# Gated mix of infini-attention and a ReGLU block: PV of two head groups in one stretch, with a new order of all instructions

## The chip, the cores and the metric

The kernel runs on one core of a Trainium2 chip. A core has five engines with instruction queues of their own: PE (matmuls; its weight loads are listed apart as PEld), ACT (ScalarE), DVE (VectorE), POOL (GpSimd) and SP (SyncE, which here only issues DMAs). The metric is the device time of one execution in microseconds (us), median of the runs.

## What is computed

x has 2048 tokens of 512 features. One branch is an attention with 32 heads of 16 features in four segments of 512 tokens, causal within a segment, with a compressive memory of the earlier segments; the other is a ReGLU block of width 1792. A gate per token mixes them.

```
scale, phi = 16 ** -0.5, lambda t: where(t > 0, t + 1, exp(t))
for s in range(4):                       # segments of 512 tokens; q, k, v = x@wq, x@wk, x@wv
    p     = softmax(q[s] @ k[s].T * scale + causal mask)
    a_dot = p @ v[s]                     # "PV"
    a_mem = (phi(q[s]) @ M) / (phi(q[s]) @ z + 1e-6)
    o[s]  = sigmoid(beta) * a_mem + (1 - sigmoid(beta)) * a_dot
    M, z  = M + phi(k[s]).T @ v[s], z + phi(k[s]).sum()
a = concat(o) @ wo
b = (relu(x @ W_gate) * (x @ W_up)) @ W_down
g = sigmoid((x * gate_w).sum(-1))
out = g * a + (1 - g) * b
```

## The kernel before

All data are bf16, sums in PSUM are f32. x is kept transposed on chip (xT, loaded in four chunks of 512 tokens, one per segment). For each segment there are projections (q, k, v: full 128x128 matmuls of 512 columns, L543 to L552), the score, PV, the memory, the ReGLU's wg and wu (L745) with relu (L753 on ACT, L754 on DVE) and product (hm, L756 on DVE), and the output tiles (wo, L777, and wd, L784, summed in one PSUM bank, then scaled on the way out, L793 and L794).

*Score visit* ("quad"). The 32 heads are four groups G of eight. The keys of a group stand in eight blocks c of 64 keys; a block is scored against the queries from 64c on, with four 32-row tiles of PE side by side, one per pair of heads (L653). Parts are packed so that each visit fills four PSUM banks with 512 columns: blocks 1 and 7, 2 and 6, 3 and 5, block 0 alone, and block 4 of two groups together. That gives nine visits per two groups, 72 in all. One ACT instruction (L657) takes the exponential of all four banks into a tile of E, and frees the banks for the next visit. POOL then masks the diagonal part of each block (L662, two instructions per part, 256 in all).

*PV* ("pv", L685). For one group, 128 matmuls read its E tiles and the values (vaug, and vsh, the same values shifted by 64 partitions) on 64-row tiles, into two PSUM banks. DVE transposes both banks (Tn, L695), and divides and gates (rden L702, rdg L704, ad L706), transposes back (L709 or L711), and in segments 1 to 3 adds the memory's part (L712), into oT, which wo reads.

*PSUM*: eight banks of 512 f32. Before, four (psL) belong to the score and four (psA) to everything else: a full matmul's tile takes one of them, a PV two, and is freed by its reader on ACT or DVE. *E*: eight tiles, seven in a ring and one for block 4.

*Order*. The order of every engine's instructions is written out: ORDER is a string of letters, each letter names a queue of instructions (score, PV, projections, each kind of eviction, loads and so on), and the next instruction of that queue is placed. BANKS gives the PSUM bank of each tile. Waits between engines follow from the order and from who reads and writes what. An engine runs its list strictly from the front, so an instruction that waits holds up all behind it on that engine. SP issues all loads and stores in its listed order; it also waits there.

The rows below use these names: psL/psA (ps after the change) for PSUM, E for exponentials, Tn/adT/oT for the steps behind PV, rl and hT for relu and product, osb for output tiles, Mbd for the memory.

Of the kernel before, what the change touches and what calls it, by code (L numbers as in the profile page):

```python
# [12 lines left out]

LAT = 60.0
# [10 lines left out]
    "hafgbgbgfgbgfgbgfagbfagbhhghbhhhhhihbjijbtttbttttbthhhhhbhthtijhtbttijttbttcttbttttDbttttCtbtttDtbtCbtbtFtbctIbItFbtbFJqbJtzJJtbEtxbtStGbvtGbzTvJtbMTq"  # L25
    "HtbJxvSbvSvbMvvcToqkvbLvoxtMTvbTvGTvlLvboqvoxvVMTvTvMTvTnlqVnvLoTvlxTMtWTtMmtTWtCTpqFvlSxtJtVJvTCvTtMyTVtTRqFvRtxvMTvJvpMvKTtSqzCvTTvMxTteMtrSeFTqATvx"
    "TvJetATttMeDTqJvxATtRvETvTvMyTqrAMTvxVQvAtrMUVUzATqUtAxTtpATtUtGTtHATqGvTxTvAtRtAvdHqMTtxTvATtTJttCTLqTvEKTtToxvdtvMTptCvTtSLqTErxSvAVtAtzTtTCvVTqATvM"
    "xtAdtRvEtLotdqAvpxCTtvTETvvTMKvTJqLvATxTvMvTdtMrzoqTpAvTxWvAvWMvtALTtAtHAqHvTAxTvosuPTMunTuPnpPqTuTxoXuTusuPuPTqPTOuTpJxuJTuuuXTquTxTsYuTPtPtPuTHXqTNu"
    "xYusvPuyPTuPTupTyRqXuuxSuTSvrNLTRqYuATxTJvATvvJvATvRLqvAxSuovMTvpTuMLvTqTArxuVQTvAUrUMTVBquATxuToutATpvTqSvxuATVtMTvUGvTOqVAvMTxvUAvYvJvMTKqTvoxvvMTpv"
    "TeMvTvTALvTeMqTvxTMvevBvMroeMTnqnvTxpATvvTAvovMTvATqLMvTxTvAvpMsvPtALtPTqADvTTxvPTtBtMrFTqTKJWvAxtWvAvtMvTDAtMTqTtAxtRtETvCtTtAvFtATLqTtBxtCTXttEtTsHu"  # L30
    "TPPTuPTqvXxJuJupvuMTquTxTsuTPuPtPtOTXqTGsxvPuPYPvuXyTMvTqTyRuuovxuTMpurRRqTAuxTtATuTJvtNKTuTGYTuATvouLqAprAxrQAUuUAUuBqtATxvUAtTouvHApqTAuxuuATTNuTvTB"
    "YvvMTLqTovxuMTvvuMnTqnpuToxJsuJPTuPvTPuTqTOvTvxYTMvpvMvvMTqvTxvMvsMvvTPqPTLvPTxvTvMvrMTqTAvTxvTAvMvvALTqAvxAvvMTTvMvTqTArTxMvBWAvWvTLAqTvxTAvAMTvvAvLq"
    "TAvTxMvTvTBvvMXTqvMTxTvXMTuuTquTxTuTuusvTPuPTMquxPuNXuuTqYrTxTTvAuAuTvTAuTLAqvAxuTAuuNTqYvTxTvMTvuMuTuTqrxvAuAvTuTAvTAvAqLuTxvuvNuYTuTvTMqTvMxvMvuuMTs"
    "qTPuPxTvPTuvXvMTvTvMTvTvLuqvxvMvvBvMTqvTAxuMvvNvLTvBYqrMTxTTvAvAvLTvTMvTvATLvAqAvxMvvAwMvTvBvMTwLTvTvvMvwLwrvAwAwwAwAvAwMwwAwwBwwwOwYOwwYwwwwwwOwwwYww"
    "wwwwwOwwwwwYNY"
)
BANKS = (
    "012312301230123023012302130231201320132013201301230210321032102310231023023020302013120312131213212301230213021301303120312031201201212012302301231231"
    "02020132032301230123012310231021230230120121302023023023102130213023023021"
# [31 lines left out]
class Epoch:  # L71
    _n = 0

    def __init__(self, nb=1):
        self.nb = nb
        self.group = (self,)
        Epoch._n += 1
        self.res = f"ACCep{Epoch._n}"
        self.bank = None
        self.readers = []  # L80
# [31 lines left out]
class Sched:  # L112
    ENGS = ("pe", "act", "dve", "pool", "sp")

    def __init__(self, ndma=16, nbanks=4):
# [89 lines left out]
    def place(self, op, e, banks):  # L205
        op.eng = e
        if op.ep is not None and op.ep.bank is None:
            assert op.role == "w"
            for ep in op.ep.group:
                bi = next(banks)  # L210
# [88 lines left out]
def build_kernel(nc, A_x, A_wq, A_wk, A_wv, A_wo, A_beta, W_g, W_u, W_d, gate_w, out):  # L299
# [7 lines left out]
    with contextlib.ExitStack() as stack:  # L307
        for name, shape, dt in plan(S, D, F):
            T[name] = stack.enter_context(nc.sbuf_tensor(name, shape, dt))
        PL = stack.enter_context(nc.psum_tensor("psL", [128, 4, 512], F32))  # L310
        PA = stack.enter_context(nc.psum_tensor("psA", [128, 4, 512], F32))
        for st in sc.streams:
            sc.sem[st] = stack.enter_context(nc.semaphore(f"s_{st}"))
        program(sc, nc, T, PL, PA, A_x, A_wq, A_wk, A_wv, A_wo, A_beta, W_g, W_u, W_d, gate_w, out, NSEG, KT, NF, NT, EPS, SCALE)
# [5 lines left out]
def program(sc, nc, T, PL, PA, A_x, A_wq, A_wk, A_wv, A_wo, A_beta, W_g, W_u, W_d, gate_w, out, NSEG, KT, NF, NT, EPS, SCALE):  # L320
# [5 lines left out]
    def pe(fn, occ, **k):  # L326
        k.setdefault("lat", PE_LAT)
        if k.get("role") == "w":
            k["reads"] = list(k.get("reads", ())) + [f"init{i}" for i in range(4)]
# [17 lines left out]
    def A(ep):  # L347
        return PA[:, ep.bank, :] if ep.nb == 1 else PA[:, ep.bank:ep.bank + 2, :]

    def xt(c):  # L350
        return [f"xT{c}_{kt}" for kt in range(KT)] if c else [f"xT0_{kt}{h}" for kt in range(KT) for h in range(2)]
# [32 lines left out]
    def load_x(c):  # L384
        for kt in range(KT):
            lsp.append(dma("sp", lambda e, c=c, kt=kt: e.dma_start_transpose(V.xT[:, kt, c * 512:(c + 1) * 512], A_x[0, c * 512:(c + 1) * 512, kt * 128:(kt + 1) * 128]),
                           1 << 17, occ=1350.0, writes=[f"xT{c}_{kt}"], name=f"ldx{c}_{kt}"))
# [22 lines left out]
    for c in range(2, NSEG):  # L410
        load_x(c)
        for t in lsp[-KT:]:
            t.after = 36500.0 + 76000.0 * (c - 2)
    sc.queue(3, lsp)

# [15 lines left out]
    for b in range(4):  # L431
        ds.append(dve(lambda e, b=b: e.memset(PA[:, b, :], 0.0), 500, writes=[f"init{b}"], name=f"init{b}"))
# [4 lines left out]
    def warm(m, n, k, b):  # L437
        def fn(e):
            for i in range(m):
                ins = e.matmul(PL[:, b, 0:n], lhsT=nc.const_aps.tensor(1.0, [128, 128], BF16), rhs=nc.const_aps.tensor(1.0, [128, n], BF16), start=True, stop=True)  # L440
            return ins
        return pe(fn, m * n * (0.834 if k == 0 else 0.5), writes=[f"bankL{b}"], name=f"warm{k}")

    xps, xcs = [warm(5, 512, 0, 3)], []
    for h in range(2):
        for i in (2 * h, 2 * h + 1):
            for kt in range(KT):
                def fx(e, i=i, kt=kt):
                    return e.matmul(PL[:, kt, 128 * (i % 2):128 * (i % 2) + 128], lhsT=V.hT[:, i, kt * 128:(kt + 1) * 128], rhs=V.ident[:], start=True, stop=True)  # L449
                xps.append(pe(fx, 60 if h else 85, reads=[f"hT{i}", "ident"], writes=[f"bankL{kt}"], name=f"xt{i}_{kt}"))  # L450
                if h:
                    xps[-1].after = 5400.0
        for kt in range(KT):
            src, dst = PL[:, kt, 0:256], V.xT[:, kt, 256 * h:256 * h + 256]
# [441 lines left out]
```

## Time and profile before

| what | us |
|---|---|
| median of 3 runs (lowest, highest) | 264.38 (264.2, 265.23) |
| the profiled execution: span, first to last instruction | 262.5 |
| median less span (start and end around it) | 1.9 |
| busy: PE, DVE, ACT, POOL | 254.5, 189.2, 186.2, 122.7 |

The profile is of one execution. For that execution its span is known; its own device time is taken as span plus the 1.9 us of the table. Times in the views are us from the start of the span, durations of one instruction ns. Matmuls overlap in their rows, so the distance between two starts is what a matmul takes of PE, not the length in its row. "L653" is line 653 of the kernel before.

### The profile page before, as it was taken

Reading aid. Unit: us, or ns where it says so; the run is one execution under the profiler, and the core shown is the slowest. Engines: PE = TensorE matmul, PEld = TensorE weight load, DVE = VectorE, ACT = ScalarE, POOL = GpSimd, SP = SyncE. Lnnn points to the kernel's source line nnn. Section 1 sums busy time; section 2 is a strip of 40 time slices with the busy share of each in tenths; the row PEclk is TensorE's granted clock in tenths of the full one; section 3 lists DMA queues with packets and bytes.
Section 4 is the critical chain, followed back from the end, with each engine's and each line's share of the span. In section 5 each row is a group of like instructions: output and inputs, shape, how many; then the busy total and the mean of one; then the engine's idle time right before and its main releaser. Section 6 shows DMA issues by size and latency. Waiting matters only on the chain.

```text
span 262.5 us, 6602 instructions
## 1 busy us (share of the span) xinstructions
PE 254.5 (97%) x2727; PEld 115.2 (44%) x2761; DVE 189.2 (72%) x365; ACT 186.2 (71%) x163; POOL 122.7 (47%) x283
## 2 busy tenths in 40 slices
PE   8999999999999999999999999999999999999996
PEld 4644344434444444434444444444434444444444
DVE  4589878888894697888785898758973665577600
ACT  3698889888886977877876957777876755674021
POOL 3017645862655546845444456535654543343000
DMA  6999621342642312431212211010231000000011
GB/s 195 274 329 216 135 59 29 83 159 46 218 107 43 82 42 49 94 82 22 57 33 60 61 45 40 20 24 4 46 81 21 31 13 20 20 22 0 2 40 42
DMA packets 34685, 19.36 MB, mean 74 GB/s; under 512 B 24032, under 2 KB 34144, under 8 KB 34656
## 3 DMA queue, kind: packets, MB, share of 16 engines
q1 hardware_dynamic: 34272, 18.67, 27.7%
q8 instruction: 22, 0.36, 0.6%
q10 hardware_dynamic: 384, 0.27, 0.3%
q14 instruction: 7, 0.06, 0.1%
HBM read 9.87 MB, written 2.11 MB: 46 GB/s over the span
## 4 chain that ended last, share of the span: by engine, by line
PE 94%; issue 2%; DMA 1%; ACT 1%; SPq 0%; DVE 0%
PE psA L745 37%; PE psA L784 19%; PE psA L552 9%; PE psL L653 9%; PE psA L685 7%; PE psA L550 5%; PE psA L777 5%; PE psA L543 1%; DMA wq<-in_A_wq_dram 1%; PE psA L615 1%; ACT E L657 1%; PE psA L595 1%; SPq L356 0%; PE psL L449 0%; DVE osb L793 0%
## 5 line engine op out<-in xcount | busy, mean ns | idle before, releaser
L662 POOL TENSOR_SCALAR_AFFINE_SELECT E<-E 64x256 bf16<-64x256 bf16 (+1 forms) x256 | 115.0, 459 | 115.0 <-ACT E L657 106.5
L657 ACT ACTIVATE E<-psL 128x2048 bf16<-128x2048 f32 x72 | 135.1, 1876 | 33.3 <-PE psL L653 32.9
L745 PE MATMUL psA<-xT,wu 128*128 128x512 bf16 x214 | 59.2, 380 | 1.6 <-issue 1.4
L745 PE MATMUL psA<-xT,wg 128*128 128x512 bf16 x213 | 59.0, 380 | 1.6 <-issue 1.4
L784 PE MATMUL psA<-wd,hT 128*128 128x512 bf16 (+2 forms) x232 | 57.6, 367 | 0.7 <-issue 0.6
L756 DVE TENSOR_TENSOR hT<-psA,rl 128x512 bf16<-128x512 f32 x56 | 38.0, 682 | 15.1 <-PE psA L745 11.2
L784 PEld LDWEIGHTS psA<-wd,hT 128*128 128x128 bf16 x238 | 21.4, 98 | 24.3 <-issue 2.8
L745 PEld LDWEIGHTS psA<-xT,wu 128*128 128x128 bf16 x224 | 19.8, 98 | 25.2 <-issue 4.1
L745 PEld LDWEIGHTS psA<-xT,wg 128*128 128x128 bf16 x224 | 20.1, 98 | 24.4 <-issue 2.8
L695 DVE STREAM_TRANSPOSE Tn<-psA 128x512 f32<-128x512 f32 x32 | 21.4, 698 | 11.0 <-PE psA L685 10.7
L653 PE MATMUL psL<-qT,kp 32*128 32x192 bf16 (+7 forms) x512 | 28.6, 287 | 0.0
L753 ACT ACTIVATE rl<-psA 128x512 bf16<-128x512 f32 x29 | 17.3, 596 | 15.0 <-PE psA L745 14.8
L754 DVE TENSOR_SCALAR rl<-psA 128x512 bf16<-128x512 f32 x27 | 18.5, 686 | 5.8 <-PE psA L745 5.6
L653 PEld LDWEIGHTS psL<-qT,kp 32*128 32x128 bf16 x512 | 8.3, 92 | 27.0 <-issue 9.3
L685 PE MATMUL psA<-E,vaug 64*17 64x128 bf16 (+7 forms) x512 | 18.7, 283 | 0.0
L685 PE MATMUL psA<-E,vsh 64*17 64x128 bf16 (+7 forms) x512 | 18.3, 283 | 0.0
L550 PE MATMUL psA<-wv,xT 128*128 128x512 bf16 x62 | 16.7, 379 | 0.2 <-issue 0.2
L552 PE MATMUL psA<-xT,wk 128*128 128x512 bf16 x62 | 16.7, 379 | 0.1
L777 PE MATMUL psA<-wo,oT 128*128 128x512 bf16 (+2 forms) x66 | 16.0, 366 | 0.3 <-issue 0.3
L794 ACT ACTIVATE osb<-psA,omg 128x512 bf16<-128x512 f32 (+1 forms) x8 | 5.4, 673 | 14.4 <-PE psA L777 13.1
L793 DVE TENSOR_SCALAR osb<-psA,omg 128x512 bf16<-128x512 f32 (+1 forms) x9 | 6.3, 701 | 12.5 <-PE psA L777 10.4
L685 PEld LDWEIGHTS psA<-E,vaug 64*17 64x17 bf16 x512 | 11.6, 86 | 7.7 <-issue 1.9
(73 smaller groups left out, 234.5 us busy)
## 6 DMA issues: line engine op xcount, KB each, us to landing
vsh<-vaug SPq DMA_DIRECT2D x8, 272.0 KB, 3.8
out_dram<-osb SPq DMA_DIRECT2D x15, 128.0 KB, 1.7
wg<-in_B_W_gate_dram SPq DMA_DIRECT2D x8, 224.0 KB, 5.9
wu<-in_B_W_up_dram SPq DMA_DIRECT2D x8, 224.0 KB, 6.3
osb<-in_A_x_dram SPq DMA_DIRECT2D x12, 128.0 KB, 2.3
wd<-in_B_W_down_dram SPq DMA_DIRECT2D x3, 512.0 KB, 4.5
wq<-in_A_wq_dram SPq DMA_DIRECT2D x4, 128.0 KB, 3.3
wk<-in_A_wk_dram SPq DMA_DIRECT2D x4, 128.0 KB, 3.5
```

The source lines that it names most:

```text
L550: ins = e.matmul(A(ep)[:, :], lhsT=V.xT[:, kt, tok + col * 128:tok + (col + 1) * 128], rhs=w[:, kt, :], start=(kt == 0), stop=(kt == KT - 1))
L552: ins = e.matmul(A(ep)[:, :], lhsT=w[:, kt, col * 128:(col + 1) * 128], rhs=V.xT[:, kt, tok:tok + 512], start=(kt == 0), stop=(kt == KT - 1))
L653: ins = q.matmul(PL[:, jj, o:o + 512 - 64 * c], lhsT=V.kp[r, kslot(s, G), c, :], rhs=V.qT[r, qslot(s, G), 64 * c:512], start=True, stop=Tr ...
L657: acts.append(act(lambda a: a.activation(V.E[:, e, :, :], PL[:, :, :], ACT.Exp, scale=SCALE), t_act(2048), reads=[f"bankL{b}" for b in ran ...
L662: pools.append(pool(lambda g, ap=ap, base=base: g.affine_select(out=ap, in_=ap, compare_op=ALU.is_ge, fill=0.0, base=base, pattern=[[0, 4] ...
L685: ins = q.matmul(A(eps[p])[32 * jj:32 * jj + 17, 64 * c:512], lhsT=v[:, 8 * G + 2 * jj + p, :], rhs=V.E[r, e, jj, o:o + 512 - 64 * c], sta ...
L695: ds.append(dve(lambda e, p=p, ep=eps[p]: e.transpose(V.Tn[:, p, :], A(ep)[:, :]), 706, writes=[f"Tn{p}"], name=f"tr{s}_{G}_{p}", ep=eps[p ...
L745: ins = e.matmul(A(ep)[:, :], lhsT=w[:, kt, f * 128:(f + 1) * 128], rhs=V.xT[:, kt, c * 512:(c + 1) * 512], start=(kt == 0), stop=(kt == K ...
L754: ("dve", lambda e, ep=eg, r=r: e.tensor_scalar(V.rl[:, r, :], A(ep)[:, :], 0.0, None, ALU.max), t_dve(512))],
L756: evs.append(dve(lambda e, ep=eu, r=r, hs=hs: e.tensor_tensor(V.hT[:, hs, :], A(ep)[:, :], V.rl[:, r, :], ALU.mult), t_dve(512), reads=[f" ...
L777: ins = e.matmul(A(ep)[:, 0:c1 - c0], lhsT=V.oT[:, o0 + G, i * 128:(i + 1) * 128], rhs=V.wo[:, G, c0:c1], start=st_ and G == 0, stop=sp_ a ...
L784: ins = e.matmul(A(ep)[:, 0:c1 - c0], lhsT=V.hT[:, slots[f], i * 128:(i + 1) * 128], rhs=V.wd[:, f, c0:c1], start=st_ and f == f0, stop=sp ...
```

## The change

PV now works on two groups, one directly behind the other: nine score visits give the nine E tiles of two groups, and after the second visit (in the list of dependences) of the next two groups, one stretch of 256 matmuls does PV for both, into four PSUM banks. E becomes a ring of 11 tiles. To make room on chip, xT keeps three chunks (the fourth reuses the first's place once segment 0 is done with it, and its load is issued later), kp four groups instead of five, hT 15 tiles instead of 16, and oTt goes (the memory's part is added in place in oT). PSUM is one tensor of eight banks: the score takes banks 0 to 3, and a table gives every other tile its bank, which at the start and the end may be one of those four too. The four memsets of PSUM at the start go. The order is laid out anew: ORDER names each instruction itself (two letters each) and the engine that does it, so the split of evictions between ACT and DVE, the order of masks on POOL and that of loads on SP are new too.

```diff
+NE = 11
+NX = 3
+NH = 15
...
-        for x in ORDER:
-            q = self.queues[LETTERS.index(x)]
-            while q[1][q[2]].done:
-                q[2] += 1
-            self.place(q[1][q[2]], q[0], banks)
+        for i in range(0, len(ORDER), 2):
+            v = 62 * LETTERS.index(ORDER[i]) + LETTERS.index(ORDER[i + 1])
+            op = self.ops[v // 2]
+            self.place(op, op.engs[v % 2], banks)
...
-        PL = stack.enter_context(nc.psum_tensor("psL", [128, 4, 512], F32))
-        PA = stack.enter_context(nc.psum_tensor("psA", [128, 4, 512], F32))
+        PS = stack.enter_context(nc.psum_tensor("ps", [128, 8, 512], F32))
...
-    for c in range(2, NSEG):
+    for c in range(2, NX):
         load_x(c)
...
-    for b in range(4):
-        ds.append(dve(lambda e, b=b: e.memset(PA[:, b, :], 0.0), 500, writes=[f"init{b}"], name=f"init{b}"))
...
-        return (s * 4 + G) % 5
+        return (s * 4 + G) % 4
...
-        def quad(tag, parts, slot=None):
-
-            e = slot
-            if e is None:
-                e = e_ctr[0]
-                e_ctr[0] = (e + 1) % 7
+        def quad(tag, parts):
+            e = e_ctr[0]
+            e_ctr[0] = (e + 1) % NE
+            ep = Epoch(4, 0)
...
-            s, G, at = carry.pop()
-            eps = [Epoch(), Epoch()]
-            pair = []
-            mem = mu(s) if G == MU_G and s < NSEG - 1 else None
+            s, G0, at = carry.pop()
+            eps = [Epoch() for _ in range(4)]
+            for k in (0, 2):
+                eps[k].group = eps[k + 1].group = (eps[k], eps[k + 1])
+            mem = mu(s) if G0 == 0 and s < NSEG - 1 else None
...
             def fpv(q):
-                for c in range(8):
+                for g in range(2):
+                    G = G0 + g
+                    for c in range(8):
...
+            pv = [pe(half(0), 2304 / 2.4 + 50.0, reads=rd, writes=[eps[1].res], name=f"pv{s}_{G0}", ep=eps[0], role="w", mode="h")]
+            pv.append(pe(half(1), 2304 / 2.4 + 50.0, reads=rd, writes=[eps[3].res], name=f"pw{s}_{G0}", ep=eps[2], role="w", mode="h"))
...
-                ds.append(dve(lambda e: e.transpose(V.oTt[:, :], V.adT[:, :]), 702, reads=["adT"], writes=["oTt"], name=f"bt{s}_{G}"))
-                ds.append(dve(lambda e: e.tensor_tensor(V.oT[:, os_, :], V.oTt[:, :], V.amemT[:, G, :], ALU.add), 435, reads=["oTt"] + [f"amemT{i}" for i in range(4)], writes=[f"oT{os_}"], name=f"oa{s}_{G}"))
+                ds.append(dve(lambda e, os_=os_: e.transpose(V.oT[:, os_, :], V.adT[:, :]), 702, reads=["adT"], writes=[f"oT{os_}"], name=f"bt{s}_{G}"))
+                if s > 0:
+                    ds.append(dve(lambda e, os_=os_, G=G: e.tensor_tensor(V.oT[:, os_, :], V.oT[:, os_, :], V.amemT[:, G, :], ALU.add), 435, reads=[f"oT{os_}"] + [f"amemT{i}" for i in range(4)], writes=[f"oT{os_}"], name=f"oa{s}_{G}"))
...
-        for G in range(4):
-            at |= quad(f"{G}A", [(G, 0, 0)])
-            at |= quad(f"{G}B", [(G, 1, 0), (G, 7, 448)])
-            flush()
...
+        for G in range(0, 4, 2):
+            at = {}
+            for n, (tag, parts) in enumerate((("B", [(G, 1, 0), (G, 7, 448)]), ("C", [(G, 2, 0), (G, 6, 384)]), ("D", [(G, 3, 0), (G, 5, 320)]), ("A", [(G, 0, 0)]), ("E", [(G, 4, 0), (G + 1, 4, 256)]),
+                                              ("F", [(G + 1, 1, 0), (G + 1, 7, 448)]), ("G", [(G + 1, 2, 0), (G + 1, 6, 384)]), ("H", [(G + 1, 3, 0), (G + 1, 5, 320)]), ("I", [(G + 1, 0, 0)]))):
+                at |= quad(f"{G}{tag}", parts)
+                if n == NE - 10:
+                    flush()
...
+            carry.append((s, G, at))
...
+        if s + NX < NSEG:
+            load_x(s + NX)
+            for t in lsp:
+                t.after = 95000.0
```

Three places of the order. The first is PE in segment 0 around PV of the second group (before): the last rows of that PV (17 columns of output, E with vsh and vaug), the score visit behind it (psL<-qT,kp), and what stands between the next score visits, which is v (L550), wu and wg (L745).

```order
L685 MATMUL psA<-E,vsh 17x64 x4
L685 MATMUL psA<-E,vaug 17x64 x4
L653 MATMUL psL<-qT,kp 128x256 x8
L550 MATMUL psA<-wv,xT 128x512 x10
L653 MATMUL psL<-qT,kp 128x384 x4
L653 MATMUL psL<-qT,kp 128x128 x4
L745 MATMUL psA<-xT,wu 128x512 x4
L550 MATMUL psA<-wv,xT 128x512 x4
L745 MATMUL psA<-xT,wg 128x512 x2
L653 MATMUL psL<-qT,kp 128x320 x4
```

PE in the changed kernel, in the second PV stretch of segment 0, where the first group's last blocks meet the second group's first.

```order
L693 MATMUL ps<-E,vaug 17x128 x4
L693 MATMUL ps<-E,vsh 17x128 x4
L693 MATMUL ps<-E,vsh 17x64 x4
L693 MATMUL ps<-E,vaug 17x64 x4
L693 MATMUL ps<-E,vaug 17x512 x4
L693 MATMUL ps<-E,vsh 17x512 x4
```

And PE behind the same stretch, up to the third score visit.

```order
L693 MATMUL ps<-E,vsh 17x64 x4
L693 MATMUL ps<-E,vaug 17x64 x4
L660 MATMUL ps<-qT,kp 128x320 x4
L660 MATMUL ps<-qT,kp 128x192 x4
L559 MATMUL ps<-wv,xT 128x512 x2
L756 MATMUL ps<-xT,wg 128x512 x2
L559 MATMUL ps<-wv,xT 128x512 x2
L756 MATMUL ps<-xT,wg 128x512 x2
L660 MATMUL ps<-qT,kp 128x512 x4
L559 MATMUL ps<-wv,xT 128x512 x10
L660 MATMUL ps<-qT,kp 128x256 x8
```

Before, each group's PV stood in a stretch of its own, and ten matmuls stood between the next score visits; now two groups' PV meet, and eight full matmuls stand between the visit behind them and the next.

The second place is DVE behind the PV of segment 0's third group (before; Tn<-psA are the two transposes of its banks):

```order
L502 ISA osb,gl<-osb,gwb 128x512
L502 ISA gl 128x1
L695 STREAM_TRANSPOSE Tn<-psA 128x512 x2
L756 TENSOR_TENSOR hT<-psA,rl 128x512
L702 RECIPROCAL rden<-Tn 128x32
L704 TENSOR_TENSOR rdg<-rden,gexpT 128x32
L706 TENSOR_TENSOR adT<-Tn,rdg 128x2x16x16
L709 STREAM_TRANSPOSE oT<-adT 128x512
```

and behind the stretch of the third and fourth (after):

```order
L512 ISA osb,gl<-osb,gwb 128x512
L512 ISA gl 128x1
L714 STREAM_TRANSPOSE Tn<-ps 128x512 x2
L718 RECIPROCAL rden<-Tn 128x32
L720 TENSOR_TENSOR rdg<-rden,gexpT 128x32
L722 TENSOR_TENSOR adT<-Tn,rdg 128x2x16x16
L714 STREAM_TRANSPOSE Tn<-ps 128x512 x2
L718 RECIPROCAL rden<-Tn 128x32
L724 STREAM_TRANSPOSE oT<-adT 128x512
```

Two transposes and one chain became four transposes with the first group's chain between them, since Tn holds two banks.

The third place is SP's first loads, behind x and wq, before

```order
L356 DMA wk<-in_A_wk_dram 128x512 x4
L356 DMA wv<-in_A_wv_dram 128x512 x4
L356 DMA wg<-in_B_W_gate_dram 128x896 x4
L356 DMA wu<-in_B_W_up_dram 128x896 x4
L356 DMA braw<-in_A_beta_dram 128x32
L356 DMA gwb<-in_gate_w_dram 128x512
```

and after:

```order
L366 DMA wk<-in_A_wk_dram 128x512 x3
L366 DMA wv<-in_A_wv_dram 128x512
L366 DMA wk<-in_A_wk_dram 128x512
L366 DMA wg<-in_B_W_gate_dram 128x896
L366 DMA braw<-in_A_beta_dram 128x32
L366 DMA wv<-in_A_wv_dram 128x512 x2
L366 DMA wu<-in_B_W_up_dram 128x896
L366 DMA wv<-in_A_wv_dram 128x512
L366 DMA wg<-in_B_W_gate_dram 128x896 x2
L366 DMA gwb<-in_gate_w_dram 128x512
```

One wg, braw and one wu moved ahead of the last wv.

More of the change, by code (lines that the diff above doesn't have):

```diff
@@ L209, in place @@
             for ep in op.ep.group:
-                bi = next(banks)
+                bi = next(banks) if ep.fix is None else ep.fix
                 for i in range(bi, bi + ep.nb):
@@ L409, in program @@
     lsp = []
-    for c in range(2, NSEG):
+    for c in range(2, NX):
         load_x(c)
-        for t in lsp[-KT:]:
-            t.after = 36500.0 + 76000.0 * (c - 2)
+        for t in lsp:
+            t.after = 32000.0
     sc.queue(3, lsp)
+    lsp = []
     st = []
@@ L690, in flush @@
                 rd += [f"E{e}"] + [f"E{e}m{b}{i}" for b in (0, 64) for i in range(2)]
-            pair.append(pe(fpv, 2304 / 2.4 + 40.0, reads=rd, writes=[eps[1].res], name=f"pv{s}_{G}", ep=eps[0], role="w", mode="h"))
-            if mem:
-                pair.insert(0, mem[0])
-            for p in range(2):
-                ds.append(dve(lambda e, p=p, ep=eps[p]: e.transpose(V.Tn[:, p, :], A(ep)[:, :]), 706, writes=[f"Tn{p}"], name=f"tr{s}_{G}_{p}", ep=eps[p], role="r"))
-            for t in pair[1:]:
-                pair[0].preds += [d for d in t.preds if d not in pair[0].preds]
@@ L698, in flush @@
-            pvs.extend(pair)
-            Tv = V.Tn[:, :, :].rearrange("q p (c r) -> q p c r", r=32)
-            rv = V.rden[:, :].rearrange("q (p c) -> q p c", p=2)
-            gv = V.rdg[:, :].rearrange("q (p c) -> q p c", p=2)
-            ds.append(dve(lambda e: e.reciprocal(rv, Tv[:, :, :, 16]), 345, reads=["Tn0", "Tn1"], writes=["rden"], name=f"rden{s}_{G}"))
-            ge = V.gexpT[:, 16 * s:16 * s + 16].rearrange("q (a t) -> q t a", t=4).unsqueeze(1).to_broadcast([128, 2, 4, 4])
-            ds.append(dve(lambda e: e.tensor_tensor(gv.rearrange("q p (t a) -> q p t a", a=4), rv.rearrange("q p (t a) -> q p t a", a=4), ge, ALU.mult), 215, reads=["rden"] + gexpT_r[s], writes=["rdg"], name=f"rdg{s}_{G}"))
@@ L713, in flush @@
[L713 to L727 removed]
+            it = []
@@ L857, in program @@
     sc.queue(1, Q["spo"])
+    sc.queue(3, lsp)
     sc.run()
```

184 lines of the change are left out of this document (99 added, 85 removed).

## The prediction

> **What bounds the kernel now.** I read the page from the top: busy time by engine, the 40 slices, the chain that ended last.
>
> ```profile
> span 262.5 us, 6602 instructions
> PE 254.5 (97%) x2727; PEld 115.2 (44%) x2761; DVE 189.2 (72%) x365; ACT 186.2 (71%) x163; POOL 122.7 (47%) x283
> PE   8999999999999999999999999999999999999996
> PE 94%; issue 2%; DMA 1%; ACT 1%; SPq 0%; DVE 0%
> ```
>
> PE is busy in every slice and is 94% of the chain. The span is 262.5, the median of the runs 264.38, so 1.9 us lie around the span; I keep those and work on the span. The view of PE's waits, of the array and of its weight loads (us in total, times, longest), says whether anything holds it up:
>
> ```profile
> PE psA L745 <- issue: 2.9, 18, 0.2
> PE psL L440 <- PEq L881: 0.8, 1, 0.8
> PEld psA L543 <- DMA wq<-in_A_wq_dram: 0.6, 1, 0.6
> ```
>
> Beyond the first microseconds no engine and no DMA keeps PE's matmuls waiting; what is left are "issue" pieces of 0.2. So only PE's own work, or a new wait, can change the time. Where PE's time goes beside its matmuls is seen in the timeline, in a piece with a lone score visit (L653) and a PV stretch (L685) followed by a score visit:
>
> ```profile
> 114.47 1.03 PE L745 MATMUL psA<-xT,wu 128*128 128x512 bf16 x4
> 115.43 0.40 PE L653 MATMUL psL<-qT,kp 32*128 32x448 bf16 x8
> 115.76 1.04 PE L745 MATMUL psA<-xT,wg 128*128 128x512 bf16 x4
> 115.88 1.88 ACT L657 ACTIVATE E<-psL 128x2048 bf16<-128x2048 f32 x1 [0.61 <-PE psL L653]
> 116.63 1.03 PE L745 MATMUL psA<-xT,wu 128*128 128x512 bf16 x4
> 117.59 0.39 PE L685 MATMUL psA<-E,vaug 64*17 64x512 bf16 x4
> 118.69 0.40 PE L653 MATMUL psL<-qT,kp 32*128 32x384 bf16 x8
> 119.02 0.55 PEld L745 LDWEIGHTS psA<-xT,wg 128*128 128x128 bf16 x4 [0.21 <-issue]
> ```
>
> Four full matmuls take 116.63 - 115.76 = 0.87, so one of 512 columns takes 0.2165. The four of 114.47 end at 115.34, and the score visit starts at 115.43: **0.10 to change** from full matmuls to the score's 32-row tiles. A score visit is four row tiles of 512 columns side by side, 0.2165; the next full matmul starts at 115.76, so **0.11** to change back. Into PV: 116.63 + 0.87 = 117.50 to 117.59, 0.10 again. One PV streams 512+448+...+64 = 2304 columns, 4.5 times 512, 0.97; the score visit behind it starts 1.10 after PV, **0.13** out of PV.
>
> **The change, part by part.** *Shapes on PE.* The matmuls are the same in number and shape, and so are the 72 score visits. What differs is how often PE changes shape. Counted in the two orders (before, after): full to score 63, 65; score to full 64, 69; full to PV 10, 4; PV to score 9, 7; PV to full 7, 1; score to PV 5, 1; with the three memory updates, which also have a shape of their own, 6 and 6 more. In all 164 and 153. At the prices above: +2 x 0.10 + 5 x 0.11 - 6 x 0.10 - 2 x 0.13 - 6 x 0.13 - 4 x 0.11 = -1.33; the three updates move by hundredths. **-1.35.** This lies on PE, so all of it counts. The trace has no place where one group's PV follows another's. Bounds: 0 as between the 64-column and other blocks inside one PV, whose sum above leaves no gap, and 0.23 (out of PV and in again) at each of 8 seams, +1.9 in all. I take 0, the nearer row, since the tiles keep their shape.
>
> *The start.* The four memsets of PSUM on DVE go; they ended long before PE had x, so nothing is gained. The loads on SP are mixed: a wg, the beta row and a wu now stand ahead of the last wv.
>
> ```profile
> 5.54 1.85 SPq L356 DMA_DIRECT2D wv<-in_A_wv_dram  x4
> 11.33 0.70 SPq L356 DMA_DIRECT2D braw<-in_A_beta_dram  x1
> wv<-in_A_wv_dram SPq DMA_DIRECT2D x4, 128.0 KB, 3.7
> wg<-in_B_W_gate_dram SPq DMA_DIRECT2D x8, 224.0 KB, 5.9
> 6.87 2.56 PE L543 MATMUL psA<-xT,wq 128*128 128x256 bf16 x22
> ```
>
> An issue takes 1.85 / 4 = 0.47, so the last wv was issued at 6.97 and now at 6.97 + 2 x 0.47 + 0.70 = 8.6. It lands 3.7 later at 12.3, or 5.9 later at 14.5 if it fares like a wg. PE wants it for the second half of the first v tile. From 5.52, where wq's wait ends, PE then does 26 q matmuls of 0.11 (2.56 / 22, the first ones slower), 8 transposes a quarter as long as a full matmul, 16 k and 2 v of 0.2165: some 7.5, so at 13.0. The wait is 0 to 1.5; I take 0, by wv's own row.
>
> *One short gap.* The exponential frees the four score banks; a visit can't start before. From a visit to its exponential 115.88 - 115.43 = 0.45, and that takes 1.88: 2.33 from visit to visit. With n full matmuls between, PE comes after 0.2165 + 0.11 + 0.2165 n + 0.10: 2.59 for n = 10, as in
>
> ```profile
> 52.82 0.40 PE L653 MATMUL psL<-qT,kp 32*128 32x320 bf16 x8
> 53.27 1.88 ACT L657 ACTIVATE E<-psL 128x2048 bf16<-128x2048 f32 x1 [0.17 <-PE psL L653]
> 55.41 0.39 PE L653 MATMUL psL<-qT,kp 32*128 32x512 bf16 x4
> ```
>
> and 2.16 for n = 8. Before, 10 was the smallest spacing of two plain visits and came 20 times; now it comes 42 times, and 8 once (the wv row between two visits, in the order above). There PE waits 0.17 and the hand-over: **+0.2** (0.15 to 0.3). The visits 10 apart have 0.26 to spare, room for ACT to do one more short piece, not two.
>
> *Who evicts.* In ACT's and DVE's lists 10 relus and, net, 7 copies and output tiles leave ACT, and 10 and 7 arrive on DVE, which loses its four memsets.
>
> ```profile
> L754 DVE TENSOR_SCALAR rl<-psA 128x512 bf16<-128x512 f32 x27 | 18.5, 686 | 5.8 <-PE psA L745 5.6
> L695 DVE STREAM_TRANSPOSE Tn<-psA 128x512 f32<-128x512 f32 x32 | 21.4, 698 | 11.0 <-PE psA L685 10.7
> L706 DVE TENSOR_TENSOR adT<-Tn,rdg 128x512 bf16<-128x512 f32 x16 | 12.4, 776 | 0.3
> L702 DVE RECIPROCAL rden<-Tn 128x32 f32<-128x32 f32 x16 | 5.5, 346 | 0.2
> L704 DVE TENSOR_TENSOR rdg<-rden,gexpT 128x32 f32<-128x32 f32 x16 | 5.2, 323 | 0.2
> ```
>
> DVE goes from 189 to about 199 us, 76%: not the bound, but its queue is what frees PSUM. Worst is the PV stretch: its four banks are all that full matmuls have beside the score's four, and DVE must transpose each before PE reuses it. Behind the first half of a stretch DVE does two transposes, reciprocal, gate product, ad, a third transpose: 3 x 0.698 + 0.346 + 0.323 + 0.776 = 3.54, starting 0.2 after that half. In the same time PE does the second half with its change (1.10), a visit and its change (0.33), 8 matmuls (1.73), the change, the late visit and back (0.2 + 0.43): 3.8. Even; what is queued ahead of the transposes on DVE (a gate, 763 ns before) decides. **+0.1** (0 to +1.5 over the eight stretches). Behind a late transpose stand the ad chain and the next hm, for which wd matmuls wait much later.
>
> *Masks.* PV reads 9 tiles of exponentials that POOL has masked, 32 masks, where it read one group's before.
>
> ```profile
> L662 POOL TENSOR_SCALAR_AFFINE_SELECT E<-E 64x256 bf16<-64x256 bf16 (+1 forms) x256 | 115.0, 459 | 115.0 <-ACT E L657 106.5
> L604 POOL TENSOR_TENSOR Mbd<-Mc,mumask 128x136 bf16<-128x136 f32 x12 | 5.7, 487 | 3.4 <-DVE Mc L600 3.4
> 100.00:120.00 20.00, 11.69 (x24) 1.00 0.36 81
> 20.00:240.00 220.00, 111.79 (x250) 1.00 0.26 61
> ```
>
> (The last two are windows with the masks alone.) In the new order of POOL the masks of a pair are mixed, and at several pairs a mask of the fifth tile stands near the front, so POOL stands idle until that tile's exponential. In segment 1's second pair, 32 masks and 3 Mbd products then remain before PV: 32 x 0.459 + 3 x 0.487 = 16.15. PE has there 6 visits of 0.43 and 76 matmuls, 19.0, less the 2.33 until the exponential is done: 16.7. Half a microsecond to spare, gone at 0.475 a mask; 100 to 120 us shows 11.69 / 24 = 0.487, the whole 111.79 / 250 = 0.447. I take **+0.3** for all stretches; bounds 0 and +3.
>
> *Free edits.* The fourth x chunk's loads now wait for segment 0's last use of x and stand in SP's queue among segment 0's stores; PE has segment 1's wg and wu until it needs them, and only a store held up ahead of them would make a q tile late. Adding in place instead of through oTt keeps the same two DVE instructions. The tail has the same last matmuls, and DVE's eviction of 384 columns there lies under the 18 matmuls behind it.
>
> **Sum:** -1.35 + 0 + 0.2 + 0.1 + 0.3 = -0.75. Span 261.7, time **263.6**.
>
> **Rivals.** *Clean:* no new wait bites, as none did before; only shapes and the short gap count, -1.2 to -1.35: 263.0. For it: PE's wait rows; against: less slack everywhere (42 spacings of 10).
>
> *Masks late (slower):* POOL becomes the bound ahead of the PV stretches, from 0.475 a mask on. At 0.505, a tenth over the mean, segment 1's second pair is late by 32 x 0.046 - 0.5 = 1.0; four such stretches and the rest of the sum give 264.38 - 1.05 + 4 = 267.3, two give 265.3; I price it at 266.4. For it speaks
>
> ```profile
> L662 POOL TENSOR_SCALAR_AFFINE_SELECT E<-E x256: 406/416/952, 15.4 to 241.4; 64x256 bf16<-64x256 bf16 x128
> ```
>
> a median of 416 ns but single masks up to 952; against it that the mean counts masks whose starts overlap, and 0.447 leaves 0.9. The Trainium skill (SBUF — State Buffer, section "Who interferes with whom") says that a DVE instruction with two SBUF inputs and a GpSimd instruction that reads SBUF exclude each other for the whole instruction; the long masks here fit that, and by that rule masks bunched beside ad and the gates would go this way.
>
> *DVE late:* eviction queues at the stretches, +1.5 on the clean case's 263.0: 264.5 to 265.
>
> *The seam costs a change of shape:* the double stretch saves nothing; 263.6 + 1.9 = 265.5.
>
> **Chances.** Forecast 0.43, clean 0.22, masks late 0.17, DVE late 0.13, seam 0.05. The range reaches from the clean case with a slightly better start, 262.7, over DVE late and seam to the milder half of masks late, 266.2. Half a per cent, about what a measurement of this kernel can tell from no change, is 1.3 us: faster means below 263.06, which is most of the clean case, 0.2; slower above 265.70, masks late and a little more, 0.18; within, 0.62.
>
> **What would show it.** Right: PE's changes of shape at 0.10 to 0.13, PV stretches of 2.05 to 2.1 us with no gap at the seam, a single wait of 0.2 of a score visit on the exponential near 75 us, no wait of L693 (PV) on POOL. Wrong: rows of PE or its weight loads waiting for POOL's masks, for DVE's transposes or hm, or for the wv or wu loads in the first 25 us; each microsecond of these is one of time.

## The result, and the profile after

The changed kernel takes **272.73 us** (median of 5 runs, 272.21 to 274.33) against 264.38 before: a ratio of 1.0328, 95% interval 1.0302 to 1.0354. It is 8.35 us slower, where 263.6 was forecast. The page of its profile, top lines, the code transfers of part 3 and the chain by engine:

```profile
span 270.5 us, 6592 instructions
PE 256.5 (95%) x2730; PEld 116.9 (43%) x2761; DVE 200.3 (74%) x378; ACT 175.3 (65%) x146; POOL 113.9 (42%) x283
PE   8999999899898998989999989999999999999996
q8 instruction: 21, 0.34, 0.5%
PE 80%; DVE 8%; SPq 5%; issue 3%; DMA 2%; ACT 1%
```

PE does the same 2761 weight loads with their matmuls, but six more slices have fallen under 90%, and DVE and SP's queue are now in the chain. The view of PE's waits (us in total, times, longest):

```profile
PE ps L660 <- issue: 2.3, 2, 1.3
PE ps L756 <- DVE hT L767: 1.5, 3, 0.7
...
PE ps L788 <- issue: 1.1, 1, 1.1
...
PE ps L693 <- issue: 1.0, 1, 1.0
...
PE ps L561 <- DVE hT L767: 0.3, 1, 0.3
PE ps L756 <- DMA wu<-in_B_W_up_dram: 0.2, 1, 0.2
```

Three kinds can be told apart. I went through PE's rows in order, from one change of shape to the next, and took from each piece the time that its kind usually takes; what is left over sums like this (us of the span):

| where in the changed kernel | us |
|---|---|
| pauses without a named cause behind or in the PV stretches at 47, 102 and 158 us | 1.6 + 1.2 + 1.2 = 4.0 |
| waits for hT, rl and output tiles from DVE at 64, 67 to 70, 114, 117 and 176 us | 2.8 |
| wo's first matmul at 82 (wd's load), and wu's piece at 21.5 us | 1.3 + 0.3 |
| start 0.2, transposes and short gap at 75 us 0.2 | 0.4 |
| changes of shape and seams | -0.8 |
| sum (270.5 - 262.5 = 8.0) | 8.0 |

*The pauses.* The timeline of PE at the first:

```profile
46.42 0.24 PE L693 MATMUL ps<-E,vsh 64*17 64x128 bf16 x8
46.62 0.39 PE L660 MATMUL ps<-qT,kp 32*128 32x320 bf16 x5
48.36 0.26 PE L660 MATMUL ps<-qT,kp 32*128 32x192 bf16 x3 [1.35 <-issue]
48.78 0.81 PE L756 MATMUL ps<-xT,wg 128*128 128x512 bf16 x3 [0.16 <-issue]
```

PE stops in the middle of a score visit, after five of its eight matmuls. Only the first has anything to wait for, so no buffer explains this.

*DVE.* Its timeline before the waits near 64 and 67 to 70 us, and windows (us, busy by engine) of the same ten microseconds after and before:

```profile
61.04 1.46 DVE L720 TENSOR_TENSOR rdg<-rden,gexpT 128x32 f32<-128x32 f32 x1
62.42 0.70 DVE L724 STREAM_TRANSPOSE oT<-adT 128x512 bf16<-128x512 bf16 x1
...
65.05 1.44 DVE L542 TENSOR_TENSOR ek<-ek,ttmp 128x1024 bf16<-128x1024 bf16 x1
66.42 0.89 DVE L722 TENSOR_TENSOR adT<-Tn,rdg 128x512 bf16<-128x512 f32 x1
...
60.00:70.00 10.00, 8.98 (x55) 3.33 (x54) 9.57 (x17) 8.13 (x8) 9.65 (x23) 1.00 0.10 28
```

```profile
60.00:70.00 10.00, 9.68 (x119) 4.26 (x98) 8.95 (x18) 8.47 (x8) 5.15 (x12) 1.00 0.60 172
```

The fifth number pair is POOL: 9.65 of 10 us busy with 23 instructions, where it was 5.15 with 12. In that burst rdg, 0.32 in the mean before, takes 1.46, while the transpose between, with one input, keeps its 0.70. POOL's own timeline shows where the burst comes from: it stood 4 us behind a mask of a late tile, then worked without a break.

```profile
52.85 1.14 POOL L668 TENSOR_SCALAR_AFFINE_SELECT E<-E 64x256 bf16<-64x256 bf16 x3
57.96 4.05 POOL L668 TENSOR_SCALAR_AFFINE_SELECT E<-E 64x256 bf16<-64x256 bf16 x9 [3.97 <-ACT E L664]
...
63.17 5.58 POOL L668 TENSOR_SCALAR_AFFINE_SELECT E<-E 64x256 bf16<-64x256 bf16 x11
```

*SP.* Its timeline (issue rows) ahead of wo's first matmul at 83.15:

```profile
42.27 26.21 SPq L509 DMA_DIRECT2D osb<-in_A_x_dram  x3
...
70.62 1.13 SPq L366 DMA_DIRECT2D wd<-in_B_W_down_dram  x2
...
77.47 0.58 SPq L366 DMA_DIRECT2D wd<-in_B_W_down_dram  x1
```

From 42.27 to 68.48 SP issues three small x rows for the gates and nothing else: the second and third each wait until DVE's gate has read the row before. wo and wd stand behind them, and the last wd piece lands 5.6 us after its issue, at 83.06.

### The profile page after: what moved, and what is told of

It reads as the page before. It is cut to its first block, busy times and chain, and to the rows that moved or that the text cites. A ratio compares the mean times of both kernels' runs of the same rounds, so it can differ in the third digit from the quotient of the medians.

```text
span 270.5 us, 6592 instructions
## 1 busy us (share of the span) xinstructions
PE 256.5 (95%) x2730; PEld 116.9 (43%) x2761; DVE 200.3 (74%) x378; ACT 175.3 (65%) x146; POOL 113.9 (42%) x283
## 4 chain that ended last, share of the span: by engine, by line
PE 80%; DVE 8%; SPq 5%; issue 3%; DMA 2%; ACT 1%
PE ps L756 31%; PE ps L795 18%; PE ps L660 8%; PE ps L561 7%; PE ps L693 6%; PE ps L788 5%; SPq L366 4%; PE ps L559 4%; DMA wu<-in_B_W_up_dram 2%; DVE hT L767 1%; PE ps L624 1%; SPq L396 1%; DVE osb L512 1%; DVE ek L542 1%; ACT E L664 1%
## 5 line engine op out<-in xcount | busy, mean ns | idle before, releaser
L664 ACT ACTIVATE E<-ps 128x2048 bf16<-128x2048 f32 x72 | 135.1, 1877 | 48.3 <-PE ps L660 47.8
L756 PE MATMUL ps<-xT,wg 128*128 128x512 bf16 x218 | 58.8, 380 | 2.0 <-DVE hT L767 1.5
L756 PE MATMUL ps<-xT,wu 128*128 128x512 bf16 x216 | 57.7, 380 | 1.4 <-issue 0.8
L795 PE MATMUL ps<-wd,hT 128*128 128x512 bf16 (+2 forms) x228 | 54.6, 366 | 1.4 <-issue 1.3
L767 DVE TENSOR_TENSOR hT<-ps,rl 128x512 bf16<-128x512 f32 x56 | 37.8, 683 | 14.4 <-PE ps L756 14.2
L756 PEld LDWEIGHTS ps<-xT,wg 128*128 128x128 bf16 x224 | 20.3, 98 | 27.9 <-DVE hT L767 3.5
L795 PEld LDWEIGHTS ps<-wd,hT 128*128 128x128 bf16 x238 | 21.3, 98 | 24.5 <-issue 3.4
L765 DVE TENSOR_SCALAR rl<-ps 128x512 bf16<-128x512 f32 x37 | 24.6, 683 | 9.2 <-PE ps L756 9.1
L660 PE MATMUL ps<-qT,kp 32*128 32x512 bf16 (+7 forms) x512 | 29.1, 287 | 2.5 <-issue 2.3
L714 DVE STREAM_TRANSPOSE Tn<-ps 128x512 f32<-128x512 f32 x32 | 21.5, 699 | 4.9 <-PE ps L693 4.6
L693 PE MATMUL ps<-E,vsh 64*17 64x64 bf16 (+7 forms) x512 | 17.5, 283 | 1.0 <-issue 1.0
L693 PE MATMUL ps<-E,vaug 64*17 64x128 bf16 (+7 forms) x512 | 17.8, 283 | 0.0
L693 PEld LDWEIGHTS ps<-E,vaug 64*17 64x17 bf16 x512 | 12.6, 86 | 3.2 <-issue 0.4
```

The source lines that it names most:

```text
L660: ins = q.matmul(PS[:, jj, o:o + 512 - 64 * c], lhsT=V.kp[r, kslot(s, G), c, :], rhs=V.qT[r, qslot(s, G), 64 * c:512], start=True, stop=Tr ...
L664: acts.append(act(lambda a: a.activation(V.E[:, e, :, :], PS[:, 0:4, :], ACT.Exp, scale=SCALE), t_act(2048), writes=[f"E{e}"], name=f"exp{ ...
L693: ins = q.matmul(A(eps[2 * g + p])[32 * jj:32 * jj + 17, 64 * c:512], lhsT=v[:, 8 * G + 2 * jj + p, :], rhs=V.E[r, e, jj, o:o + 512 - 64 * c],
L714: ds.append(dve(lambda e, p=p, ep=eps[2 * (G - G0) + p]: e.transpose(V.Tn[:, p, :], A(ep)[:, :]), 706, writes=[f"Tn{p}"], name=f"tr{s}_{G} ...
L756: ins = e.matmul(A(ep)[:, :], lhsT=w[:, kt, f * 128:(f + 1) * 128], rhs=V.xT[:, kt, c % NX, :], start=(kt == 0), stop=(kt == KT - 1))
L765: ("dve", lambda e, ep=eg, r=r: e.tensor_scalar(V.rl[:, r, :], A(ep)[:, :], 0.0, None, ALU.max), t_dve(512))],
```

## The experiments

The names in the diffs are those of the instructions in the code; ORDER was changed to match.

**1 and 2: shift the code.** The idea: PE's program is brought in by transfers of 16 KB (0.34 MB in 21 on queue q8 of the page), and counted along its trace PE has 5574 instructions (a weight load, its matmul and a semaphore instruction are one each). That is about 62 bytes for each; I take 64, so 256 to a block. The pauses begin at instruction 961, 2240 and 3520: 193, 192 and 192 modulo 256. (Ahead of the prediction a PV is said to have 128 matmuls. It has 64, each with its weight load: 1024 rows of L693 for 16 PVs. So 128 and 256 there are instructions, and a two-group stretch alone is one block's worth of them.) The words behind # in the diff are mine.

```diff
-        for i in range(5):        # warm-up, 512 columns
+        for i in range(3):        # run shift24; 2 in shift88
...
+        for i in range(26):       # 34 columns, 32-column weights; 91 in shift88
```

> The changed kernel with 24 more matmuls in the warm-up at the start (three of 512 columns and 26 of 34 columns on 32 rows, for five of 512), so that every later PE instruction stands 48 instructions further on; nothing else differs. Theory code supply: PE's instructions come in blocks of 16 KB, 256 instructions, and the three pauses of 1.2 to 1.6 us (near 47, 102 and 158 us), which stand at 193 or 194 modulo 256 in PE's instructions, fall where a block is used up in less than about 3.5 us. Moved by 48 they become about 1.3 to 1.6 us each, earlier inside or ahead of the PV stretch, and a fourth of 1.2 to 1.5 us appears near 217 us: 5.4 to 6.2 us of pauses for 4.0, time 274 to 275. Rival, the pauses are a hand-over of PSUM banks from DVE or POOL: nothing moves, 272.7.

> As the run with 24 more, but 88 more small matmuls (two of 512 columns and 91 of 34 columns). Theory code supply: the block ends now fall 176 instructions earlier in the program, where hardly any block is used up in 3.5 us: pauses of 0.6 to 1.2 us in all for 4.0, a small one new near 182 us, time 269.4 to 270.2 if the warm-up costs no time. Rival, hand-over of PSUM banks: 272.7, with the pauses where they were.

Measured: shift24 272.68 us, shift88 271.82. In shift24 the pauses again begin at 961, 2240 and 3520, though the work there stands 24 matmuls earlier: they move into the PV stretch. Their sum is 4.3, not 5.4 to 6.2, the fourth did not come, and the start took 1.2 longer. The time alone would have fitted the rival (272.7); the places of the pauses don't. In shift88 all three are gone, as expected; a new one of 1.1 stands at 185 us (instruction 4289, 193 modulo 256), and one of 2.0 at 77 us (1729, 193 again), while wo and wd load. The time fell by 0.9 only, since the start took 2.5 longer (0.9 of it waits for x and wq) and the new pauses 3.1, the second in place of the 1.3 of wait for wd. Pauses from a hand-over of PSUM would not have moved.

**3: masks in tile order.** In POOL's list:

```diff
-mask0_2C mu16_0 mask0_2D mu16_0 mask0_2C mask0_2C mask0_2C mask0_2E mask0_2D mask0_2B
+mask0_2B mask0_2B mask0_2B mask0_2B mask0_2C mask0_2C mask0_2C mask0_2C mu16_0 mask0_2D
...
```

> The changed kernel with POOL's masks in the order of the exponentials (each tile's masks behind its own exponential), so that POOL does not stand behind a late tile and then do 20 masks without a break. Theory POOL bunches: DVE's instructions with two SBUF inputs stand still while POOL works on SBUF without a break (rdg takes 1.46 us near 61 us where the mean before was 0.32; ek's 1.44 for 0.69). With masks spread the worst of them fall below 1 us, and PE's waits for hT and rl near 64, 67 to 70, 114 and 117 us (2.3 us together) go or shrink to under 0.7: time 270.3 to 271.2. Part of the wait near 82 us may go too, since the x row behind the late gate leaves earlier. Rival, DVE is late because it has 17 more evictions: the waits stay, 272.7. Second rival: masks in tile order come too late for PV, and PE waits for POOL ahead of PV: slower.

Measured: **269.76**, 3.0 less, 0.5 below the range that I expected. The rows of the two-input instructions (min/median/max ns), of the changed kernel and of this one:

```profile
L720 DVE TENSOR_TENSOR rdg<-rden,gexpT x16: 173/213/1456, 47.5 to 257.3; 128x32 f32<-128x32 f32 x16
L542 DVE TENSOR_TENSOR ek<-ek,ttmp x6: 629/766/1444, 16.5 to 134.8; 128x1024 bf16<-128x1024 bf16 x6
L542 DVE TENSOR_TENSOR phiq<-phiq,ttmp x6: 682/1164/1781, 41.3 to 209.8; 128x1024 bf16<-128x1024 bf16 x6
```

```profile
L720 DVE TENSOR_TENSOR rdg<-rden,gexpT x16: 171/212/451, 48.2 to 254.8; 128x32 f32<-128x32 f32 x16
L542 DVE TENSOR_TENSOR ek<-ek,ttmp x6: 628/684/758, 17.1 to 132.4; 128x1024 bf16<-128x1024 bf16 x6
L542 DVE TENSOR_TENSOR phiq<-phiq,ttmp x6: 681/682/766, 42.0 to 207.3; 128x1024 bf16<-128x1024 bf16 x6
...
60.00:70.00 10.00, 9.95 (x67) 3.90 (x67) 8.55 (x19) 8.60 (x9) 8.18 (x17) 1.00 0.27 44
110.00:120.00 10.00, 9.95 (x61) 4.07 (x61) 8.93 (x17) 8.77 (x8) 7.39 (x16) 1.00 0.35 65
```

The long ones are gone, PE is back at 9.95 of 10 us in both windows, and DVE still has its 17 added evictions: by themselves they don't make PE wait. The Trainium skill (SBUF — State Buffer, "Who interferes with whom") has this rule: a DVE instruction with two SBUF inputs contends with a GpSimd instruction that reads SBUF, and the shared ports are locked by one of them and not split; rdg's 1.46 against a median of 0.21 agrees. So do the masks of the kernel before: each of the 26 that took over 0.65 us overlaps a DVE instruction with two inputs in SBUF. The wait for wd shrank from 1.3 to 0.4, since the gates came earlier. Waits of 0.4 for a wg and 1.1 for a wu piece appeared near 16 and 21 us.

**4: loads earlier.** SP's list:

```diff
 ldwu0_2
+ldwu0_3
 ldwu1_2
...
 ldxr4
+ldwo ldwd0 ldwd4 ldwd8 ldwd12
 ldxr5
```

> The changed kernel with two changes in SP's order: the last wu piece of the first half ahead of the four loads that stand before it, and wo and the four wd loads ahead of the second x row for the gates (whose issue waits for DVE's gate at 59 us), so that they are issued from 43 us on. Theory SP queue: the 1.3 us of wait near 82 us is wd's and wo's loads, issued only after 70 us, and the 0.3 us near 21.5 us is wu's: both go, time 271.1. Rival: the wait near 82 us is for the copy of v on ACT or the transposes on DVE ahead of wo's matmuls: it stays, 272.4. If 2.3 MB of loads from 43 to 52 us slow the code blocks, the pause near 47 us grows from 1.35.

Measured: **276.37**, slower by 3.6. The waits at 21.5 and 82 us went as expected, but the pause at 47 us grew from 1.6 to 4.9 and cost more behind it. The timeline, and windows during the pause and behind it (last three numbers: granted clock of PE, DMA share, GB/s):

```profile
51.14 0.34 PE L660 MATMUL ps<-qT,kp 32*128 32x192 bf16 x3 [4.58 <-issue]
...
46.00:51.10 5.10, 0.56 (x37) 0.20 (x15) 2.62 (x6) 1.00 (x2) 0.34 (x1) 0.88 0.99 325
51.10:56.00 4.90, 4.53 (x13) 1.70 (x14) 0.96 (x2) 2.37 (x2) 0.23 (x1) 0.50 0.03 9
```

The 2.3 MB kept the DMA engines at 0.99 while the code block was due: the block's transfer started 4.5 us after PE entered the block before it (48.59 and 44.05 in the trace), where the changed kernel had 1.5 (45.97 and 44.50). PE stopped at 46.6; the trace has its clock at 1.00 until 49.9, 3.3 us into the pause, and at 0.50 from there to 56.7. Against the same matmuls of the changed kernel that cost 2.6 us more. Of the four executions one took 273.24, with a clock of 1.00 in the mean; the other three (276.26 to 276.87) had 0.987 or 0.988. The Trainium skill (TensorE: Matmul & The Clock Gate, "HAM oscillation — how this bites in real kernels") warns of PE gaps above about 3.4 us; the clock here fits that, and the pause of some 2 us in the run masks left it at 1.00.

**5: both good parts.** masks, and of loads only ldwu0_3.

> The run masks (269.8) with one load more moved: the last wu piece of the first half ahead of the four loads before it. Theory SP queue: masks shows a wait of 1.1 us for this piece near 21 us; it goes, 268.7. Rival, the early loads are bound by the bytes of the transfers and not by their order: another piece is late instead, 269.8.

Measured: 268.07. The wu wait is gone, and the pauses came out at 3.3 us for 4.5 in masks, which is the rest of the gain. They and wd's wait of 0.8 are what is left.

**6 to 8: waits that are already over as filler.** A dictionary gives PE instructions ahead of which reached semaphores are waited for:

```diff
+                        if e == "pe":
+                            for i in range(2 * PAD.get(n, 0)):
+                                engobj.wait_ge(self.sem[f"dma{i}"], 16)
+                            n += 1
```

> The run combo with 480 more PE instructions, all waits on semaphores that were reached long before, spread between full matmuls (176 from 14 to 43 us, 32 from 75 to 95, 96 from 102 to 122, 144 from 127 to 149, 32 from 155 to 176), so that no block of 256 PE instructions is used up in less than about 4 us. Theory code supply: the three pauses (4.5 us in the run masks) go and no new ones come: 264.2 to 264.9. Rival, hand-over of PSUM banks: 268.7 as combo. Second rival, the added waits are not hidden beside the matmuls: at 51 ns each up to 24 us slower.

> The kernel before with 96 more PE instructions of that kind between full matmuls from 14 to 43 us; nothing else. Theory code supply: PE's instructions stand 96 further on, and no block is used up in under 4 us in this place: no pause, 264.4 as before. It is the control for the next run: if the added waits cost time by themselves, it shows here.

> The kernel before with 192 such instructions in the same stretch. Theory code supply: blocks now end so that the memory update, its PV and the PV and score visits behind use one up in 1.6 to 2.5 us near 104 and 159 us: pauses of 0.3 to 0.9 and 1.6 to 2.2 us, 266.3 to 267.4, in a kernel whose work and order are untouched. Rival, the pauses belong to the two-group PV stretch itself: 264.4.

Measured: aligned 271.04, bpad96 264.48 and bpad192 264.89 (before on that chip 264.31). bpad96 shows that filler is free where it stands thin (two of these waits make one instruction); twice as much in bpad192 cost 0.6 at most. The other two missed. aligned lost the pause at 158 us, but has three again, at instructions 961, 1728 and 2240 (193, 192, 192 modulo 256), the second of 4.3 us:

```profile
PE ps L772 <- issue: 3.8, 1, 3.8
```

It falls at 75 us in the wo and wd loads, and behind it the clock stood at 0.50 for 3.4 us. bpad192 has no pause where 1.6 to 2.2 were expected. So I had the condition wrong: there PE used up a block in 1.9 us (157.3 to 159.2), but the transfer of the next had started 0.4 us before PE entered it.

Put together, the traces say this of the 26 pauses of over 0.7 us in the changed kernel and the runs made from it (those below among them). In all 26, PE goes on 2.2 to 2.9 us after the transfer of its next block has started. In 21 that is 3.3 to 4.3 us after PE entered the block before. In the other five it is 5.3 to 7.7 us, because the transfer started late, 2.9 to 4.9 us after that entry; the DMA engines were busy for 0.4 or more of that time (in the 21, for 0 to 0.66).

What PE's request for a block waits for is not seen. In dense stretches the times fit a request some 32 instructions ahead of the block's entry, with the transfer about 1 us later, which makes 3.5 us for 288 instructions. Ahead of slower stretches they don't: in pad164 the transfer for the pause at 180 us starts 3.8 us after that point, with DMA nearly idle. By this count the tightest block of the kernel before, and of bpad192, had 3.5 us, at the edge. Wherever the block ends fall, the tightest 288 instructions of the kernel before take 3.0 us (by the starts of the weight loads), those of the changed kernel 1.8: that is what the change made denser.

**9 to 12: loads in a free place, and filler by the corrected rule.** loads2 is combo with the five loads behind ldxr5; aligned2, pad164 and pad208 add 728, 164 and 208 waits.

> The run combo (268.1) with wo and the four wd loads moved in SP's order to behind the second x row for the gates, so that they are issued at 58 to 61 us, where full matmuls and single score visits run, and not at 66 to 75. Theory SP queue: combo's wait of 0.6 to 0.8 us near 79.5 us is wd's last piece; it goes, and the loads meet no dense stretch of PE's instructions as they did in the run loads: 267.2 to 267.4. Rival, any moved bulk load delays a code block: a pause near 67 or 72 us, 268 or more.

> The run loads2 with 728 satisfied waits spread between full matmuls (192, 176, 104, 32, 184, 24 and 16 in seven stretches), so that the block ends, which were at 193 modulo 256 in every pause so far, fall near the middle of each stretch of memory update, PV and scores, and the bulk loads fall where no block is near its end. Theory code supply, with a block at hand 3.5 us after PE is 32 instructions from the end of the one before: all three pauses (3.5 us with combo's) go: 263.4 to 264.2, no pause over 0.3 us. Rival, blocks are late wherever DMA queues are busy: a pause of 1 to 2 us stays near 45 or 101 us, as in the run aligned, 265 to 267.

> The run loads2 (267.8) with only 164 satisfied waits, all between 15 and 43 us, at most four ahead of two full matmuls. Theory code supply: every later block end stands 164 instructions earlier in the program, the stretches of memory update, PV and scores no longer hold two block ends within 3.5 us, and all three pauses (3.7 us in loads2) go with a quarter of the waits of the run aligned2, whose waits cost some 1.5 us where six stood together: 264.1 to 264.6. If a block takes 5 us where other transfers run, 0.3 to 1.2 us of pauses stay (near 45, 95 and 177 us): up to 265.5. Rival, the pauses went in aligned2 because the added waits gave DVE and POOL time: with no wait added after 43 us the pauses near 97 and 152 us stay, 266.5.

> As pad164 with 208 waits in the same stretch. Theory code supply: the block ends fall near the middle of the dense stretches; pauses 0 at 3.5 us a block, and at 5 us a block 1.0 us near 71, 123 and 154 us in place of those of pad164: 264.1 to 265.3; the added waits cost 0.2 more than in pad164. Rival as in pad164: 266.5.

Measured: loads2 267.79, aligned2 266.48, pad164 266.46, pad208 265.77. loads2 lost wd's wait, but its pauses sum to 3.7 where combo's are 3.3, so that 0.3 of the gain is seen. In aligned2 no pause is left, as expected, but 5 or 6 waits in a row ahead of a matmul pair cost 1.5 us near 130 us, and it missed 263.4 to 264.2. pad164 keeps pauses of 0.8 and 1.5 (and 0.3 near 96 us), pad208 one of 1.4, again at 192 or 193 modulo 256: the blocks took 3.6 to 3.7 us from PE's entry into the one before. pad164's time is that of the rival that waits had given DVE time (266.5), but this rival falls by the places: with none added after 43 us, the pause at 152 us is gone in both, and that at 97 us shrank to 0.3 or went.

**13: filler that is work.** loads2, with 116 pairs of full matmuls in halves of 256 columns:

```diff
+    def matmul(self, out, lhsT, rhs, start, stop):
+        self.q.matmul(out[:, 0:256], lhsT=lhsT, rhs=rhs[:, 0:256], start=start, stop=False)
+        return self.q.matmul(out[:, 256:512], lhsT=lhsT, rhs=rhs[:, 256:512], start=False, stop=stop)
```

> The run loads2 with 116 pairs of full matmuls issued as halves of 256 columns (51 pairs from 15 to 43 us, 36 from 47 to 71, 29 from 75 to 97): the same work in 464 more PE instructions, since half a matmul takes half the time (0.11 for 0.2165 us), where pad164 and pad208 spent waits that cost 0.2 to 0.9 us of their own and kept a pause of 1.5 us. Theory code supply: block ends fall as in pad208, and off the stretch near 73 us too; no pause over 0.5 us. If code, SP's queue and POOL's bunches are all that the forecast lacked, its own terms are left: 1.3 us fewer changes of shape less 0.5 for the eight seams, 0.2 for the short gap and 0.2 at DVE there: 263.6 to 264.3. Rival, something else of the change costs time (the shapes save nothing): 265.0 or more.

Measured: **264.62**, ratio 1.0010, interval 0.9999 to 1.0021: the time of the kernel before. Its page:

```profile
span 262.6 us, 7060 instructions
PE 255.7 (97%) x2966; PEld 139.6 (53%) x2993; DVE 195.9 (75%) x378; ACT 175.4 (67%) x146; POOL 121.1 (46%) x283
PE   8999999999999999999999999999999999999996
```

No pause is left, and PE is at 90% or more in all slices but the first and the last, as before. So what was added against the three causes takes back 8.1 of the 8.35 us. It is 0.3 above the upper end that I expected. Halves are not quite free: two starts lie 0.109 apart, so two halves take 0.218 for 0.2165, some 0.35 us on 232 matmuls (worked out, not measured alone), about what is missing. No version beat the kernel before.

## Why the prediction was wrong

- *What bounds the kernel:* right for before, and it misled. "Only PE's own work, or a new wait, can change the time" is true, but I read "no wait shows" as slack on every supply line. Code had none: 3.5 us for its tightest block, about what such a block takes.
- *Shapes, -1.35, seams at nothing:* the sign was right and the size off. The timeline of a two-group stretch (first matmul of PV, first of the visit behind):

```profile
73.10 0.39 PE L693 MATMUL ps<-E,vaug 64*17 64x512 bf16 x4
...
75.24 0.40 PE L660 MATMUL ps<-qT,kp 32*128 32x320 bf16 x8
```

  2.14 us, less twice 0.974 and the 0.13 out of PV, leaves 0.06 for the seam, 0.5 in eight. -1.35 + 0.5 = -0.85 fits the -0.8 of the table.
- *Start, 0 (0 to 1.5):* 0.5. wv came in time; the wu piece moved behind the x chunk was late by 0.3.
- *Short gap, +0.2:* about right, 0.2 together with the transposes ahead of it.
- *Masks late for PV, +0.3:* PV waited for none. The step looked at the wrong end. I had seen that POOL would stand behind a late tile and then bunch its masks, but priced only longer masks. DVE pays as well.
- *DVE, +0.1 (0 to 1.5), and the rival "DVE late":* 2.8. The mechanism named, more evictions queued at the stretches, does not make PE wait by itself (run masks); DVE was late because its two-input instructions grew beside POOL's burst. The price was out of range.
- *"Free edits":* failed at "only a store held up ahead of them". I followed the x chunk through SP's queue and not wo and wd, which the new order put behind two x rows that wait for DVE's gates: 1.3.
- *What was missing altogether* is the largest term, 4.0: the supply of PE's instructions. The memory update, two PVs and two visits are 416 instructions (208 weight loads and their matmuls) in some 3 us. The page shows code transfers of 16 KB, so that two block ends can fall within that stretch was to be read from it. That no trace of before had a pause was no bound on the price of a denser stretch.

## What to carry to other kernels

Count instructions, not only time: where an engine runs hundreds of tiny instructions in a few microseconds, divide by the block of its code transfers (here 256), and ask for some 3.5 to 4.5 us a block, 5 to 8 beside heavy loads. When an engine's order is laid out anew, look for places where it first stands idle behind one late input and then works without a break, and ask which other engine's instructions grow longer meanwhile. Follow every load in an issuing queue past the first instruction that waits for a computation.

## What was unexpected of the hardware

- All 26 pauses of over 0.7 us without a named cause, in the changed kernel and the runs made from it (at 961, 1728, 1729, 2240, 3520 and 4289), begin at 192 or 193 modulo 256 of PE's instructions. When PE asks for a block is not seen; the start of the transfers gives it only in part.
- A two-input DVE instruction of 0.21 us took up to 1.46 beside a POOL that never rests; spreading the same masks brought the longest to 0.45.
- Half-size matmuls are almost free. Waits that are over cost nothing measurable at one or two ahead of two full matmuls (96 in bpad96), at most 0.6 us in all at three or four (192 in bpad192), and 1.5 us where five or six stand together (aligned2).
